# Two small changes in a fused attention and feed-forward kernel: eight early matmuls grouped by weight matrix, and the last half group of outputs cut into quarters

## The chip, the cores and the metric

One core of a Trainium2 chip; times are compared within one call, on one chip, unless it is said otherwise. The metric is device time in microseconds (us) of one execution. All executions compared here are fast, with a granted tensor-engine clock of 0.998 to 1.0. "Span" is the part of an execution that the profile covers; it is about 1.8 us shorter than the time.

## The reference

```python
def _attn_ref(q, k, v, g_norm):              # 8 batches, 8 heads, 576 tokens, head size 64
    kv = np.einsum('bhsd,bhse->bhde', k, v)
    out = np.einsum('bhsd,bhde->bhse', q, kv)
    rms = np.sqrt(np.mean(out * out, axis=-1, keepdims=True) + 1e-06)
    return (out / rms * g_norm).astype(np.float32)

def _moe_ref(x, w_a, w_b, w_out):            # 4608 tokens, width 512, inner width 1536
    a = x @ w_a
    b = x @ w_b
    return (a * b @ w_out).astype(np.float32)
# reference: x = attention output, heads side by side; result = _moe_ref(x, ...)
```

## The kernel before

Tokens go in 9 strips of 512. For each strip, 12 *units* (one per 128 columns of the inner width) each make four matmuls with w_a and four with w_b, one per K chunk of 128; ACT copies the a half to SBUF and DVE multiplies it with the b half. Then four groups of 12 matmuls with w_out make the outputs of 128 tokens each. The attention of later batches is spread between these matmuls. The contents of K chunk n of x are the heads 2n and 2n+1 ("pair n") of the attention.

POOL issues all loads of weights and of q, k and v, in the order of need. Everything up to batch 1 goes into buffers of its own:

```python
    for p in range(2, NP):
        load_pair(0, p)                       # q, k, v of a pair of heads of batch 0
    WC = 256
    for c in range(0, KC, 2):                 # first 256 columns of w_a, w_b: chunks 0-1, then 2-3
        for w, src in ((wa_t, wa_v), (wb_t, wb_v)):
            nc.gpsimd.dma_start(out=w[:, c : c + 2, 0:WC], in_=src[:, c : c + 2, 0:WC])
    for i in range(1, d_ff // WC):
        load_ab(i * WC, (i + 1) * WC)         # next 256 columns of both
    for i in range(FC):
        load_o(i)                             # w_out, 12 pieces
    for p in range(NP):
        load_pair(1, p)                       # batch 1
    load_late(2)
```

The start of the units, where the first part of the change lies (`first` is `mm(wa_t)` then `mm(wb_t)`; `rest` is `part_a` then `part_b`; `part_a` ends with the copy by ACT, `part_b` with the product by DVE):

```python
    u0 = Unit(0, 0, 2, 3)
    u1 = Unit(0, 1, 4, 5)
    u0.first((0, 1))
    A.pss(3, SS, (0,))
    A.pst(3, X[1], (0,))                      # x of pair 3, first half of the tokens, by DVE
    u1.mm(wa_t, (0,))
    A.pss(3, SS, (1,))
    A.pst(3, X[1], (1,))                      # second half
    u1.mm(wa_t, (1,))
    u1.mm(wb_t, (0, 1))
    u0.first((2,))
    u1.first((2,))
    u0.rest((3,))
    u1.rest((3,))
    u2 = Unit(0, 2, 0, 1)                     # "the next unit" below; takes columns 256 on
    ...
    ffn_o(0, 0, X[0])                         # first output group of strip 0
    pieces = [(1, h1), (1, h2), (2, h1), (2, h2), (3, h1), (3, h2)]
    for n, (g, fcs) in enumerate(pieces):     # half groups of output between the pairs of batch 1
        o_mm(0, g, O, fcs, halves=halves)
        ...
        if n < NP:
            A.qtr(n, 2)                       # transposes of q (line 200)
            A.kv(n) ...                       # K-times-V products of pair n (line 176)
```

And the end, the second part:

```python
    o_mm(last, 3, 5, range(FC), 0, hw)        # first half (256 columns) of the last group
    nc.vector.tensor_copy(o_sb[3][:, 0:hw], P[:, 5, 0:hw])
    store(r0, o_sb[3], 0, hw)                 # SP queue
    o_mm(last, 3, 6, range(FC), hw, d_model)  # second half
    nc.scalar.copy(o_end, P[:, 6, hw:])
    nc.scalar.dma_start(out=out[r0 : r0 + 128, hw:], in_=o_end)
```

Of the kernel before, what the change touches and what calls it, by code (L numbers as in the profile page):

```python
# [8 lines left out]
FP32 = mybir.dt.float32  # L9
# [6 lines left out]
def kernel(  # L16
# [11 lines left out]
    nc = tc.nc  # L28

    B, H, S, D = q.shape  # L30
    d_model = H * D
# [3 lines left out]
    FC = d_ff // 128  # L35
# [13 lines left out]
    def sb(shape, dt, name):  # L49
        return pool.tile(shape, dt, name=name, tag=name)  # L50

    wa_t = sb([128, KC, d_ff], BF16, "wa_t")
# [33 lines left out]
    x_last = x_last.rearrange("t (j p d) -> t j p d", j=2, p=NP)  # L86
    g_all = sb([128, D], FP32, "g_all")
    o_sb = [sb([128, d_model], FP32, f"osb{i}") for i in range(4)]
    o_end = sb([128, d_model // 2], FP32, "o_end")
    ident = sb([128, 128], BF16, "ident")  # L90
    ones = sb([128, 128], BF16, "ones")
    zeros = sb([128, STRIP], BF16, "zeros")
# [15 lines left out]
    P = psum.tile([128, 8, STRIP], FP32, name="P", tag="P")  # L108
# [48 lines left out]
    def product(o, lhsT, rhs, halves=False, **kw):  # L157
        for r in (slice(0, D), slice(D, 2 * D)) if halves else (slice(0, 2 * D),):
            nc.tensor.matmul(o[r], lhsT=lhsT[:, r], rhs=rhs, **kw)  # L159
# [236 lines left out]
    def store(t0, t, e0, e1, eng=nc.sync):  # L396
        i = 0
        while i < 128:
            b, j = divmod(t0 + i, S)
            if b < EARLY:  # L400
                c, p = divmod(j, EP)
                n = min(128 - i, EP - p)
                r0 = b * S + EC * p + c
                o = out[r0 : r0 + EC * (n - 1) + 1 : EC, e0:e1]
            else:
                n = min(128 - i, S - j)
                o = out[t0 + i : t0 + i + n, e0:e1]
            eng.dma_start(out=o, in_=t[i : i + n, e0:e1])
            i += n
# [3 lines left out]
    def o_mm(s, g, i, fcs, e0=0, e1=d_model, halves=False):  # L413
        for fc in fcs:
            product(
                P[:, i, e0:e1],
                abt[s % 2][fc][:, g * 128 : (g + 1) * 128],
                wo_t[:, fc, e0:e1],
                halves,
                start=(fc == 0),  # L420
                stop=(fc == FC - 1),
            )
# [98 lines left out]
    for p in range(1, NP):  # L521
        i = X[p % 2]
# [16 lines left out]
    u0 = Unit(0, 0, 2, 3)  # L539
    u1 = Unit(0, 1, 4, 5)  # L540
# [5 lines left out]
    A.pst(3, X[1], (1,))  # L546
    u1.mm(wa_t, (1,))
    u1.mm(wb_t, (0, 1))
    u0.first((2,))
    u1.first((2,))  # L550
    u0.rest((3,))
    u1.rest((3,))

    u2 = Unit(0, 2, 0, 1)
    u3 = Unit(0, 3, 2, 0)
# [33 lines left out]
    u0 = Unit(1, 0, 2, 3)  # L589
    u1 = Unit(1, 1, 4, 5)  # L590
# [55 lines left out]
    last = N_STRIP - 1  # L646
# [4 lines left out]
    hw = d_model // 2  # L651
    r0 = last * STRIP + 3 * 128
    o_mm(last, 3, 5, range(FC), 0, hw)
    nc.vector.tensor_copy(o_sb[3][:, 0:hw], P[:, 5, 0:hw])
    store(r0, o_sb[3], 0, hw)
    o_mm(last, 3, 6, range(FC), hw, d_model)
    nc.scalar.copy(o_end, P[:, 6, hw:])  # L657
    nc.scalar.dma_start(out=out[r0 : r0 + 128, hw:], in_=o_end)


# [28 lines left out]
```

## Time and profile before

| | before |
|---|---|
| time, median of 3 (range) | 313.72 us (313.65 to 313.87) |
| span of the profiled execution | 311.8 us |
| PE busy | 305.7 us, 98% |
| chain that ended last | PE 85%, DMA 8%, POOL 5% |
| first w_b matmul of chunk 2 | waits, starts at 16.65 us |
| line 176 of pairs 1 and 3 of batch 1 | start at 41.98 and 46.57 us |
| last copy by ACT | starts at 308.57 us |

PE is TensorE, PEld its weight loads. The chain that ended last is followed back from the last instruction, each time to what released it. It is the view to look at first here: PE is nearly always busy, but the chain tells where its work decides the time and where it merely fills the wait for something else. The lines themselves stand in the prediction.

### The profile page before, as it was taken

The numbers are of one execution on the slowest core, as the hardware profiler recorded it, in microseconds if no ns is written. First come the engines' busy times: TensorE is split into PE (matmuls) and PEld (weight loads), VectorE is DVE, ScalarE is ACT, GpSimd is POOL, SyncE is SP. The second block draws the span as 40 slices with busy tenths as digits, with TensorE's granted clock in tenths as the row PEclk, the third lists the DMA queues.
The fourth block names the chain that finished last, engine by engine and source line by source line (L and its number), as shares of the span: only waits on it lengthen the run. The fifth ranks groups of instructions, "written<-read, shape, count | busy, mean of one in ns | idle before, by whom it ended". The sixth has DMA issues, their size and how long they took to land.

```text
span 311.8 us, 5260 instructions
## 1 busy us (share of the span) xinstructions
PE 305.7 (98%) x2055; PEld 145.0 (47%) x2055; DVE 140.5 (45%) x234; ACT 116.9 (38%) x231; POOL 101.2 (32%) x123
## 2 busy tenths in 40 slices
PE   7999999999999999999999999999999999999995
PEld 3444474444454444544444445444444444444443
DVE  5544335458248603484386123752782143214321
ACT  3743255354255313561564033632651233123310
POOL 8944991193364640043646300221240000000000
PEclk9999999999999999999999999999999999999999
DMA  8999999999899799045997980073021200030002
GB/s 180 197 196 199 199 190 158 227 140 162 173 175 167 105 196 165 2 97 119 174 184 113 183 164 2 19 160 109 20 50 42 103 1 0 36 101 0 0 36 101
DMA packets 94254, 36.21 MB, mean 116 GB/s; under 512 B 64918, under 2 KB 89750, under 8 KB 94230
## 3 DMA queue, kind: packets, MB, share of 16 engines
q0 software_dynamic: 59120, 18.44, 54.3%
q1 hardware_dynamic: 34642, 16.87, 23.5%
q10 hardware_dynamic: 468, 0.57, 0.7%
q8 instruction: 16, 0.26, 0.3%
q14 instruction: 8, 0.07, 0.1%
HBM read 37.78 MB, written 12.98 MB: 163 GB/s over the span
## 4 chain that ended last, share of the span: by engine, by line
PE 85%; DMA 8%; POOL 5%; issue 1%; ACT 0%; POOLq 0%
PE P L358 53%; PE P L159 29%; DMA wb_t<-in_moe_w_b_dram 6%; DMA vt<-in_v_dram 2%; PE P L176 2%; PE P L292 1%; POOL qt L119 1%; POOL wo_t L134 1%; POOL kt L119 1%; POOL vt L119 1%; POOL wa_t L477 0%; POOL wb_t L477 0%; POOL wa_t L130 0%; PE P L200 0%; ACT o_end L657 0%
## 5 line engine op out<-in xcount | busy, mean ns | idle before, releaser
L376 DVE TENSOR_TENSOR ab<-P,asb 128x512 bf16<-128x512 f32 x108 | 74.4, 691 | 103.8 <-PE P L358 100.4
L358 PE MATMUL P<-xt,wb_t 128*128 128x512 bf16 x432 | 111.8, 379 | 0.3 <-DMA wb_t<-in_moe_w_b_dram 0.3
L358 PE MATMUL P<-xt,wa_t 128*128 128x512 bf16 x432 | 111.9, 379 | 0.0
L372 ACT CAST asb<-P 128x512 bf16<-128x512 f32 x108 | 62.9, 585 | 90.4 <-PE P L358 90.4
L159 PE MATMUL P<-wo_t,ab 128*128 128x512 bf16 (+2 forms) x462 | 95.7, 374 | 0.0
L159 PEld LDWEIGHTS <-ab 128*128 128x128 bf16 (+1 forms) x462 | 43.7, 99 | 48.5
L358 PEld LDWEIGHTS <-wb_t 128*128 128x128 bf16 x432 | 41.7, 98 | 50.6 <-DMA wb_t<-in_moe_w_b_dram 0.8
L358 PEld LDWEIGHTS <-wa_t 128*128 128x128 bf16 x432 | 41.8, 98 | 49.9 <-issue 0.2
L329 POOL TENSOR_TENSOR sqt<-rst,g_all 128x512 f32<-128x512 f32 (+1 forms) x24 | 25.0, 1043 | 85.2 <-ACT rst L322 85.2
L429 ACT COPY osb<-P 128x512 f32<-128x512 f32 x17 | 9.9, 585 | 70.2 <-PE P L159 65.6
L431 DVE COPY osb<-P 128x512 f32<-128x512 f32 x18 | 12.4, 691 | 44.9 <-PE P L159 44.9
L142 POOL DMA_DIRECT2D qs<-in_q_dram x12 | 19.8, 1653 | 0.7 <-issue 0.3
L313 DVE TENSOR_REDUCE sst<-sqt 128x8 f32<-128x512 f32 (+1 forms) x24 | 16.3, 680 | 1.7 <-ACT sqt L309 1.5
L338 DVE TENSOR_TENSOR qv<-P,sqt 128x512 bf16<-128x512 f32 x18 | 12.2, 680 | 0.0
L329 POOL TENSOR_TENSOR k_x<-rst,g_all 128x512 f32<-128x512 f32 x6 | 6.3, 1043 | 18.0 <-ACT rst L322 18.0
L322 ACT ACTIVATE rst<-sst,eps_t 128x8 f32<-128x8 f32 (+1 forms) x30 | 9.0, 300 | 7.1 <-DVE sst L313 6.8
L309 ACT ACTIVATE sqt<-P 128x512 f32<-128x512 f32 x18 | 10.5, 584 | 0.1
L241 DVE SCALAR_TENSOR_TENSOR xt<-P,g_col,rs 128x288 bf16<-128x288 f32 x16 | 7.5, 511 | 5.2 <-ACT rs L231 5.2
L134 POOL DMA_DIRECT2D wo_t<-in_moe_w_out_dram x12 | 6.4, 530 | 6.7 <-DMA wb_t<-in_moe_w_b_dram 3.2
L231 ACT ACTIVATE rs<-P,eps_t 128x576 f32<-128x576 f32 (+1 forms) x9 | 6.1, 688 | 3.8 <-PE P L159 3.5
L444 PE MATMUL P<-zeros 128*128 128x512 bf16 x17 | 6.0, 482 | 1.2 <-DVE eps_t L461 1.2
L139 POOL COPY gate<-qT 1x1 bf16<-1x1 bf16 x5 | 0.9, 176 | 16.8 <-DMA qT<-qs 16.7
(71 smaller groups left out, 130.7 us busy)
## 6 DMA issues: line engine op xcount, KB each, us to landing
out_dram<-osb SPq DMA_DIRECT2D x23, 256.0 KB, 2.0
qs<-in_q_dram POOLq DMA_DIRECT2D x12, 288.0 KB, 6.7
ktl<-in_k_dram POOLq DMA_DIRECT2D x6, 512.0 KB, 9.1
vtl<-in_v_dram POOLq DMA_DIRECT2D x6, 512.0 KB, 11.2
out_dram<-osb SPq DMA_DIRECT2D x13, 128.0 KB, 2.4
wo_t<-in_moe_w_out_dram POOLq DMA_DIRECT2D x12, 128.0 KB, 5.9
wa_t<-in_moe_w_a_dram POOLq DMA_DIRECT2D x5, 256.0 KB, 9.4
wb_t<-in_moe_w_b_dram POOLq DMA_DIRECT2D x5, 256.0 KB, 10.0
```

The source lines that it names most:

```text
L134: nc.gpsimd.dma_start(out=wo_t[:, i, :], in_=wo_v[:, i, :])
L142: nc.gpsimd.dma_start(out=d[:, hs, :], in_=q[b, hs].rearrange("h t d -> t h d"))
L159: nc.tensor.matmul(o[r], lhsT=lhsT[:, r], rhs=rhs, **kw)
L309: nc.scalar.activation(sqt[c % 3][r], self.by_head(c)[r], AF.Square)
L313: nc.vector.reduce_sum(sst[c % 3][r], sqt[c % 3][r].rearrange("t j p d -> t (j p) d"), axis=mybir.AxisListType.X,)
L329: nc.gpsimd.tensor_mul(sqt[c % 3][r].rearrange("t j p d -> t (j p) d"), rst[c % 3][r].unsqueeze(2).to_broadcast([n, H, D]), g_all[r].unsqu ...
L338: nc.vector.tensor_mul(t[r].rearrange("t (p j) d -> t j p d", j=2), self.by_head(c)[r], sqt[c % 3][r])
L358: nc.tensor.matmul(self.a if w is wa_t else self.b, lhsT=w[:, kc, self.fc * 128 : (self.fc + 1) * 128], rhs=xt[:, kc, t0 : t0 + STRIP], st ...
L372: nc.scalar.copy(self.t, self.a)
L376: nc.vector.tensor_mul(abt[self.s % 2][self.fc], self.b, self.t)
L429: nc.scalar.copy(t, P[:, i, :])
L431: nc.vector.tensor_copy(t, P[:, i, :])
```

## The change

The intent of part 1: at 16 us PE stood waiting for chunks 2 and 3 of w_b although w_a's were there, so do w_a's matmuls of both units first. The intent of part 2: at the end only the last copy and the last store are exposed, so make both smaller.

```diff
-    o_end = sb([128, d_model // 2], FP32, "o_end")
+    o_end = [sb([128, d_model // 4], FP32, f"o_end{i}") for i in range(2)]
...
-    u0.first((2,))
-    u1.first((2,))
-    u0.rest((3,))
-    u1.rest((3,))
+    u0.mm(wa_t, (2,))
+    u1.mm(wa_t, (2,))
+    u0.part_a((3,))
+    u1.part_a((3,))
+    u0.part_b((2, 3))
+    u1.part_b((2, 3))
...
-    o_mm(last, 3, 6, range(FC), hw, d_model)
-    nc.scalar.copy(o_end, P[:, 6, hw:])
-    nc.scalar.dma_start(out=out[r0 : r0 + 128, hw:], in_=o_end)
+    qw = hw // 2
+    for i, copy, eng in ((6, nc.vector.tensor_copy, nc.sync), (7, nc.scalar.copy, nc.scalar)):
+        e0 = hw + (i - 6) * qw
+        o_mm(last, 3, i, range(FC), e0, e0 + qw)
+        copy(o_end[i - 6], P[:, i, e0 : e0 + qw])
+        eng.dma_start(out=out[r0 : r0 + 128, e0 : e0 + qw], in_=o_end[i - 6])
```

## The prediction

> **What bounds the kernel now.** I read the page's busy shares first, then the chain that ended last, then the order of instructions on the tensor engine (PE) in the two places that the diff touches, then the landings of the loads behind them.
>
> From the page of the kernel before, busy times and the shares of the chain by engine:
>
> ```profile
> PE 305.7 (98%) x2055; PEld 145.0 (47%) x2055; DVE 140.5 (45%) x234; ACT 116.9 (38%) x231; POOL 101.2 (32%) x123
> ...
> PE 85%; DMA 8%; POOL 5%; issue 1%; ACT 0%; POOLq 0%
> ```
>
> PE is busy 98% of the span, yet only 85% of the chain is PE. The reader should ask where the other 15% lie, because there a faster PE gains nothing. The chain of waits in order of time answers (start us, length us, what):
>
> ```profile
> 11.34 7.67 DMA wb_t<-in_moe_w_b_dram
> 19.00 0.28 issue
> 19.29 10.40 DMA wb_t<-in_moe_w_b_dram
> ...
> 36.48 5.46 DMA vt<-in_v_dram
> 41.94 0.04 issue
> 41.98 0.38 PE P L176 x12
> ...
> 298.14 10.40 PE P L159 x60
> 308.55 0.02 issue
> 308.57 0.37 ACT o_end L657
> ```
>
> Up to 41.98 us the chain is loads and their issue by POOL, none of it PE. At 41.98 the K-times-V products of pair 1 of batch 1 (line 176) start right after their v data land at 41.94. From there to 308.55 it is PE without a break worth naming, then one copy and one store.
>
> The weight loads of PE around that point (timeline, weight loads only) show that the wait is real:
>
> ```profile
> 41.35 0.43 PEld L200 LDWEIGHTS <-qt 96*64 96x64 bf16 x12
> 41.69 0.11 PEld L176 LDWEIGHTS <-kt 96*64 96x64 bf16 x1
> 41.98 0.27 PEld L176 LDWEIGHTS <-kt 96*64 96x64 bf16 x11 [0.18 <-issue]
> ```
>
> The first k weights are in at 41.69, then PE stands. In pairs 2 and 3 line 176 starts 0.27 and 0.25 us after the transposes of line 200 (43.95 to 44.22, 46.32 to 46.57); here it is 0.51 (41.47 to 41.98). So PE already loses about 0.24 us to that load.
>
> The first place of the change, in the timeline of PE:
>
> ```profile
> 15.94 0.38 PE L358 MATMUL P<-xt,wa_t 128*128 128x512 bf16 x1
> 16.65 0.39 PE L358 MATMUL P<-xt,wb_t 128*128 128x512 bf16 x1 [0.33 <-DMA wb_t<-in_moe_w_b_dram]
> 16.88 0.38 PE L358 MATMUL P<-xt,wa_t 128*128 128x512 bf16 x1
> ```
>
> Matmuls of 512 columns start every 0.216 us here, so 16.65 should have been 16.16: the wait for chunks 2 and 3 of w_b costs 0.49 us of PE time (0.33 is only the part in which the pipeline was empty).
>
> The second place, the end of the timeline:
>
> ```profile
> 308.26 0.27 PE L159 MATMUL P<-wo_t,ab 128*128 128x256 bf16 x1
> 308.57 0.37 ACT L657 COPY o_end<-P 128x256 f32<-128x256 f32 x1 [4.62 <-PE P L159]
> 308.97 0.38 ACTq L658 DMA_DIRECT2D out_dram<-o_end  x1
> ```
>
> In windows of 0.1 us the bytes of that last store run from about 309.83 to 310.30; the span ends at 311.8.
>
> **What the Trainium skill says.** "TensorE: Matmul & The Clock Gate", section "Back-to-back issue gap", gives two answers for 128 columns: N/2.4 + 2.5 ns, thus 56 ns, for a lone stream, and about 81 ns where each matmul has its own weight load. This decides whether the quarters cost PE time. The trace has six such pairs (line 505, 96x128 weights, 128 columns): their weight loads start at 6.76, 6.81, 6.87, 6.92 and 6.98, so every 55 ns. It supports the lower figure, with a short sample. The page's 131 ns for 512 columns isn't what this trace has (216 ns).
> "DMA: Bandwidth & Descriptors", section "Anatomy of one DMA — SWDGE (gpsimd) path", says that most of a transfer's fixed cost is the confirmation of the last byte, whatever its size. The trace agrees in kind for the last store: 1.5 us pass from the last byte (310.3) to the end (311.8), and halving the store won't touch them. The same page, section "Specifications", puts the least row for full rate at 512 bytes; a quarter row is exactly 128 x 4 = 512 bytes. No store of the kernel before has such rows.
>
> **Part 1, the order of chunks 2 and 3.** No instruction is added or removed on any engine: eight matmuls go from a2 b2 a2 b2 a3 b3 a3 b3 (units 0, 0, 1, 1, 0, 0, 1, 1) to a2 a2 a3 a3 b2 b3 b2 b3. In the new order four w_a matmuls start at 15.94, 16.16, 16.37 and 16.59; the first w_b one at 16.80. The w_b load was issued at 9.87 and took 6.7 us, so it lands at about 16.57 and was usable at 16.65: no wait any more. The eighth starts at 17.45 and the next unit could start at 15.94 + 8 x 0.216 = 17.67 instead of 18.18, 0.51 earlier.
> That unit takes columns 256 to 512 of w_a. They were issued at 10.58 and took 7.1, so land at about 17.68, and its weight load would stand ready at 17.45. I put its start at 17.75: the local gain is 0.43 us. The next ones are in time: the same columns of w_b land at 19.00 for 19.47.
> Then 0.43 us travels with PE through the units of strip 0, and is lost in steps. The last piece of w_out is issued at 32.57 and takes about 4.9, lands near 37.5; PE wants it at 37.81 before (35.44 + 11 x 0.216) and at 37.38 after. So about 0.3 is left. v of pair 0 of batch 1 is issued at 34.53, takes 5.2, lands at 39.73; line 176 used it at 39.74. So at most 0.05 is left. And v of pair 1 lands at 41.94 whatever PE does: POOL waits only for earlier transfers in those 42 us, never for a compute engine, and each load has a buffer of its own. PE arrives earlier and waits longer. Worth on the path: 0.00.
>
> **Part 2, the quarters.** Removed: 12 matmuls of 256 columns, one copy of 256 columns on ACT, one store of 128 KB. Added: 24 matmuls of 128 columns, two copies of 128 columns (DVE, ACT), two stores of 64 KB (SP, ACT).
> PE: the 24 matmuls of 256 columns before start from about 305.75 to 308.26, 109 ns apart, so the half to be split starts at 307.06. With 24 x 55.8 ns the last one starts at 307.06 + 23 x 0.0558 = 308.34 and, with the 218 ns of line 505's form, ends at 308.56 against 308.53: +0.03.
> First quarter: ends at 307.06 + 11 x 0.0558 + 0.22 = 307.89; DVE is free since 307.68 and needs about 0.29 (0.425 for 256 columns, 0.691 for 512); SP, free since 308.04, issues at about 308.25, bytes are through by 309.4. It is beside the second quarter and off the path.
> Second quarter, on the path: the ACT copy takes 0.372 for 256 columns and 0.212 for 64, so about 0.265 for 128: -0.11. The issue and the 0.86 us from issue to first byte stay. The bytes took about 0.47 us at about 345 GB/s between ramps; half of them 0.19 plus ramps, say 0.27: -0.20. The last 1.5 us stay.
> Sum of part 2: +0.03 - 0.11 - 0.20 = -0.28 us. Sum of both: -0.28 us, 0.1% of the time. 313.72 - 0.28 = 313.44.
>
> **Rivals.**
> First: the front gain survives, since the landings at 39.73 and 41.94 move too. For it: the chain takes its releases from semaphore events and "issue" is named for the 0.18 us at 41.98, so the release by v is inferred. Against it: landing and start agree to 0.04 us, and the DMA engines moved 190 to 200 GB/s in nearly every us from 6 to 40, so the loads have no slack to give. It would make 313.72 - 0.43 - 0.28 = 313.0.
> Second: weight loads bound the quarters at 81 ns a matmul. Then they take 24 x 0.081 = 1.94 us instead of 1.31, +0.63, and the time is about 314.05. Against it stand line 505's 55 ns and its overlapping loads (98 ns each at 55 ns spacing); for it, that only six of them were seen.
> Third: rows of 512 bytes are slower per byte, or two stores in flight delay each other, so the transfer saves nothing: 313.6. The first quarter's bytes should be gone about 0.3 us before the second's begin, which speaks against the latter.
>
> **Range and chances.** The centre is 313.4. Half of the first rival and repeats a little lower give 312.95; the third with ordinary scatter (the three runs before span 0.22 us), or a part of the second, gives 313.8. A change of 2% would be 6.3 us; all that is touched, 0.5 us at the front and the last 1.3 us of PE time with its tail, comes nowhere near it.
>
> **What would show it.** Right: the wait at 16.65 gone, the next unit at about 17.7 to 17.75 with a short wait for w_a; line 176 of pair 1 of batch 1 again at 41.9 to 42.0, with about 0.3 to 0.6 us of idle PE before it and at pair 0; the matmuls from there to the end of the same length; last quarters 55 ns apart; the ACT copy at 0.26 to 0.28 us. Wrong: line 176 of pair 1 starting near 41.5, quarters 80 ns or more apart, or a last store whose bytes take 0.4 us or more.

## The result, and the profile after

| | before | after |
|---|---|---|
| time, median of 6 (range) | 313.63 us (313.48 to 313.87) | 313.25 us (313.10 to 313.62) |
| ratio of the fast runs | | 0.9989, 95% interval 0.9976 to 1.0002 |
| span of the profiled execution | 311.8 us | 311.5 us |

A ratio here is the mean time of one kernel's fast runs over the mean of the other's from the same rounds, so it is not quite the ratio of the medians. 0.38 us by the medians is near the 0.28 us forecast, but the interval just includes 1: these repeats can't say much about a quarter of a microsecond. The traces can, because they resolve 0.01 us and because the long middle of the program takes the same time in each of them.

The chain that ended last, of the changed kernel (start us, length us, what):

```profile
11.39 7.43 DMA wb_t<-in_moe_w_b_dram
...
36.58 5.26 DMA vt<-in_v_dram
41.84 0.04 issue
41.89 0.38 PE P L176 x12
...
308.51 0.27 ACT o_end L664
```

It has the same shape. Until 41.89 us it is loads and their issue; v of pair 1 lands at 41.84 (before: 41.94) and line 176 starts 0.05 us later. So the start of the PE part moved by 0.09 us because the load landed earlier in this execution, not because PE had arrived earlier.

The reordered eight, in the timeline of PE of the changed kernel:

```profile
16.06 1.27 PE L358 MATMUL P<-xt,wa_t 128*128 128x512 bf16 x4
17.17 1.02 PE L358 MATMUL P<-xt,wb_t 128*128 128x512 bf16 x4
18.04 1.03 PE L358 MATMUL P<-xt,wa_t 128*128 128x512 bf16 x4
```

The wait for w_b is gone, and the next unit starts 1.98 us after the first of the eight (16.06 to 18.04) against 2.24 before (15.94 to 18.18). But eight matmuls at 0.216 us are 1.73 us: there is a new gap of 0.25 us among the first four, which last 1.27 us instead of 3 x 0.216 + 0.38 = 1.03. The experiments below say what it is.

The wall at 42 us shows in the weight loads of the changed kernel:

```profile
41.27 0.43 PEld L200 LDWEIGHTS <-qt 96*64 96x64 bf16 x12
41.61 0.11 PEld L176 LDWEIGHTS <-kt 96*64 96x64 bf16 x1
41.89 0.26 PEld L176 LDWEIGHTS <-kt 96*64 96x64 bf16 x11 [0.17 <-issue]
```

The first k weights are in, and PE stands until v lands, as before. The end of the timeline of the changed kernel:

```profile
307.84 0.29 DVE L664 COPY o_end<-P 128x128 f32<-128x128 f32 x1 [0.24 <-PE P L159]
...
308.51 0.27 ACT L664 COPY o_end<-P 128x128 f32<-128x128 f32 x1 [4.65 <-PE P L159]
308.81 0.38 ACTq L665 DMA_DIRECT2D out_dram<-o_end  x1
```

And the bytes of the last store in windows of 0.2 us (the columns after the window are busy time of PE, PEld, DVE, ACT and POOL, the clock, the DMA share and GB/s), first of before, then of after:

```profile
309.80:310.00 0.20, 0.00 (x0) 0.00 (x0) 0.00 (x0) 0.00 (x0) 0.00 (x0) 1.00 0.60 205
310.00:310.20 0.20, 0.00 (x0) 0.00 (x0) 0.00 (x0) 0.00 (x0) 0.00 (x0) 1.00 1.04 353
310.20:310.40 0.20, 0.00 (x0) 0.00 (x0) 0.00 (x0) 0.00 (x0) 0.00 (x0) 1.00 0.31 98
```

```profile
309.60:309.80 0.20, 0.00 (x0) 0.00 (x0) 0.00 (x0) 0.00 (x0) 0.00 (x0) 1.00 0.42 125
309.80:310.00 0.20, 0.00 (x0) 0.00 (x0) 0.00 (x0) 0.00 (x0) 0.00 (x0) 1.00 0.70 200
310.00:310.20 0.20, 0.00 (x0) 0.00 (x0) 0.00 (x0) 0.00 (x0) 0.00 (x0) 1.00 0.01 3
```

The last byte leaves about 0.3 us earlier on the clock of the execution, of which 0.09 is the earlier start at 42 us.

### The profile page after: what moved, and what is told of

The parts are those of the page before. It is cut to its first block, busy times and chain, and to the rows that moved or that the text cites. A ratio compares the mean times of both kernels' runs of the same rounds, so it can differ in the third digit from the quotient of the medians.

```text
span 311.5 us, 5288 instructions
## 1 busy us (share of the span) xinstructions
PE 306.4 (98%) x2067; PEld 145.7 (47%) x2067; DVE 140.7 (45%) x235; ACT 117.0 (38%) x231; POOL 101.2 (32%) x123
## 4 chain that ended last, share of the span: by engine, by line
PE 86%; DMA 7%; POOL 5%; issue 1%; ACT 0%; POOLq 0%
PE P L358 54%; PE P L159 29%; DMA wb_t<-in_moe_w_b_dram 6%; DMA vt<-in_v_dram 2%; PE P L176 2%; PE P L292 1%; POOL qt L119 1%; POOL wo_t L134 1%; POOL kt L119 1%; POOL vt L119 1%; POOL wb_t L477 0%; POOL wa_t L477 0%; POOL wa_t L130 0%; PE P L200 0%; POOL ident masks.py:199 0%
## 5 line engine op out<-in xcount | busy, mean ns | idle before, releaser
L159 PE MATMUL P<-wo_t,ab 128*128 128x512 bf16 (+3 forms) x474 | 95.7, 368 | 0.0
```

Of the source, the lines that this page charges most:

```text
L159: nc.tensor.matmul(o[r], lhsT=lhsT[:, r], rhs=rhs, **kw)
```

## The experiments

Theory 1: up to about 46 us the time is set by the landing of loads, which doesn't depend on PE (a *wall* below is such a load: PE waits for it, however early it comes); what part 1 wins is waited away there, and all that the change wins is the shorter tail. Rivals: the front gain survives; the walls are not loads; the tail wins nothing.

Twelve kernels were run. Executions of one kernel scatter by 0.2 to 1 us, as much as the effects, so each verdict rests on the times *and* on four starts in the trace of the profiled execution:

| kernel | first of the eight | next unit | difference | line 176, pair 1 | line 176, pair 3 | time of this execution | time less pair 3 |
|---|---|---|---|---|---|---|---|
| before | 15.94 | 18.18 | 2.24 | 41.98 | 46.57 | 313.64 | 267.07 |
| after | 16.06 | 18.04 | 1.98 | 41.89 | 46.49 | 313.26 | 266.77 |
| front_only | 16.34 | 18.08 | 1.74 | 42.00 | 46.59 | 313.64 | 267.05 |
| tail_only | 16.38 | 18.10 | 1.72 | 41.87 | 46.47 | 313.24 | 266.77 |
| noload_before | 15.93 | 17.87 | 1.94 | 41.76 | 46.51 | 313.55 | 267.04 |
| noload_front | 16.06 | 18.04 | 1.98 | 41.94 | 46.69 | 313.74 | 267.05 |
| noload2_before | 16.07 | 18.02 | 1.95 | 41.53 | 46.28 | 313.31 | 267.03 |
| noload2_front | 16.39 | 18.37 | 1.98 | 41.88 | 46.63 | 313.66 | 267.03 |
| noload2_both | 16.07 | 18.05 | 1.98 | 41.56 | 46.31 | 313.06 | 266.75 |
| noload2_chunk2 | 16.40 | 18.13 | 1.73 | 41.64 | 46.39 | 313.18 | 266.79 |
| early2 | 16.46 | 18.86 | 1.97 + 0.43 | 42.38 | 47.13 | 313.92 | 266.79 |
| late2 | 16.19 | 18.05 | 1.86 | 41.94 | 46.54 | 313.80 | 267.26 |
| tail_one_mm | 15.96 | 17.93 | 1.97 | 41.84 | 46.44 | 313.55 | 267.11 |
| o_ahead | 16.07 | 17.80 | 1.73 | 42.49 | 46.66 | 313.49 | 266.83 |

The last column is the tool: by pair 3 the loads are behind, and what follows is PE alone up to the tail. The six kernels with the old tail read 267.03 to 267.07, the six with the new one 266.75 to 266.83 (late2, with work added behind pair 3, and tail_one_mm, with a tail of its own, apart). Two things vary from one execution to the next for reasons outside the change: the start of the eight (15.93 to 16.46), and the landing of v. In the traced executions, one per kernel, they account for nearly all of the scatter of the times; the other executions have no trace, and the cause of the two was not followed further.

### front_only and tail_only: each part alone

`front_only` is before with only the reordering of the diff, `tail_only` before with only the quarters.

> Part 1 alone. Theory 1 (the loads of batch 1 set the time at 42 us, so what PE wins before is waited away): time within 0.1 us of before, line 176 of pair 1 of batch 1 starting at 41.8 to 42.0 in the trace, the unit after the reordered eight about 0.25 us earlier relative to the first w_a matmul of chunk 2 than in before. Rival (the front gain survives to the end): 0.25 us faster than before.

Measured: 313.47 us median (313.39 to 313.64, 5 runs) against 313.46 of before (313.21 to 313.62, 9 runs), ratio 1.0000 (0.9986 to 1.0014). Line 176 of pair 1 starts at 42.00, as theory 1 has it. The next unit started 0.50 us earlier relative to the first of the eight than in before, 1.74 instead of 2.24, but in this trace the first of them had itself waited for w_a (it started at 16.34 where 15.98 was due), so that everything later was ready when asked for. On the clock the next unit started 0.10 us earlier than in before (18.08 against 18.18) and line 176 of pair 1 0.02 us later.

The chain of waits names v in before and after, but not here, nor in tail_only, late2 and tail_one_mm below: there it gives the last 0.03 or 0.04 us before line 176 as "issue" and goes back along PE's own work. That v is the wall in these too is read from two other things. Line 176 of pair 1 starts 0.47 to 0.49 us after the transposes of line 200, against 0.25 or 0.26 in the kernels without batch 1's loads. And v was issued at 36.50 here and took 5.5 us, so it landed at about 42.0, where line 176 started.

> Part 2 alone. Theory 1: all of the gain, 0.25 to 0.35 us faster than before. Rival (the front carries the gain): 0.1 us or less.

Measured: 313.41 us median (313.24 to 313.51, 5 runs), ratio 0.9997 (0.9985 to 1.0010): 0.05 us by the medians, 0.09 by the means, which is a miss against the 0.25 to 0.35 expected. In the trace, however, time less pair 3 is 266.77, exactly that of the changed kernel, 0.28 to 0.30 below front_only and before. So the tail's gain is in the trace, and medians of five executions with ranges of 0.27 and 0.41 us don't resolve it. It also shows that the old order doesn't always wait at 16 us: here the eight began at 16.38, w_b was there, and the next unit started 1.72 us later with no gap.

### noload_before and noload_front: batch 1's loads taken away

Both read batch 0's q, k and v tiles in place of batch 1's, which are not loaded; batch 1's rows are wrong. Old tail in both.

```diff
-    for p in range(NP):
-        load_pair(1, p)
...
-                kk, vv, rows = kt[self.b], vt[self.b], [EP] * EC
+                kk, vv, rows = kt[0], vt[0], [EP] * EC
...
-                        qt[self.b][:, 2 * p + j, c, :],
+                        qt[0][:, 2 * max(p, 1) + j, c, :],
```

(and the same `max(p, 1)` for k and v, as pair 0 of batch 0 lies elsewhere)

> Before without the q, k and v loads of batch 1; batch 1 takes the q, k, v tiles of batch 0 that are long there, so batch 1's rows are wrong on purpose. Theory 1: the wait at line 176 goes (0.24 us at pair 1, up to 0.1 at pair 0), time 0.2 to 0.4 us below before. Rival (the release by the v load was only inferred and isn't the cause): same time as before.

Measured: 313.85 us median (313.20 to 314.20, 5 runs), ratio 1.0008 (0.9996 to 1.0021): no gain, so as a prediction of the time it failed. The wait at pair 1 did go (41.50 to 41.76 is 0.26 us from the transposes, against 0.51 in before). The chain of waits of noload_before shows what took its place:

```profile
32.39 5.46 DMA wo_t<-in_moe_w_out_dram
37.85 0.04 issue
37.89 0.38 PE P L159
```

The last piece of w_out lands at 37.85, and PE waits for it there. In before that piece was issued at 32.57 and took about 4.9 us, so it landed at about 37.5, in time for the 37.8 at which PE wanted it. Here PE wanted it earlier, at 37.5 (35.14 + 11 x 0.216), and it took 5.5 us. So this is not a wall that had stood hidden in before: PE came earlier and the piece came later. The edit itself may have had a part in the latter, because it also moved later loads forward: the first q of batch 2 was issued at 41.50 in before, and at 33.08 here, right behind the last piece of w_out. Whether that slowed the piece isn't shown.

> The same with part 1 alone added. Theory 1: with those loads gone the front gain reaches the end, 0.25 us below noload_before. Rival (the gain is lost at some other wait, for example the K and V loads of batch 2 near 60 us): the same as noload_before.

Measured: 313.71 us median (313.20 to 313.86, 5 runs), ratio 1.0005 (0.9993 to 1.0018). Within the scatter equal to noload_before, which looks like the rival, but the rival named K and V of batch 2 near 60 us, and the trace has the wait at w_out again (the piece was issued only at 32.94, took 5.1 us and landed at 38.03; the matmul starts at 38.08).

### noload2_before, noload2_front, noload2_both, noload2_chunk2: both walls taken away

As above, and strip 0 takes w_out chunks 0 to 3 in place of 8 to 11, so that it needs no late piece (strip 0 is wrong as well; all of w_out is still loaded, and batch 2's loads come as early as in noload_before):

```diff
-                wo_t[:, fc, e0:e1],
+                wo_t[:, fc if s else fc % 8, e0:e1],
```

> As noload_before, and strip 0 takes w_out chunks 0 to 3 in place of 8 to 11, so that it doesn't need the last pieces of w_out either (strip 0 and batch 1 wrong on purpose; all of w_out is still loaded). In the two runs without batch 1's loads PE waited for the last piece of w_out at 37.9 to 38.1 instead. Theory 1, widened (any load that ends near 38 to 42 us is a wall for PE): the waits from 37 to 47 us go and the time falls by 0.25 to 0.4 us below before. Rival (the walls aren't loads): same as before.

Measured: 313.20 us median (312.99 to 313.31, 5 runs) against 313.53 of before (313.17 to 313.96, 9 runs), ratio 0.9988 (0.9976 to 1.0001). 0.33 us less by the medians, within the 0.25 to 0.4 expected, though the interval just includes 1. In the profiled execution the part between the next unit and pair 3 took 28.26 us against 28.39 in before, and the next unit itself came 0.16 us earlier, as w_b landed sooner. So the walls are these loads, but only 0.13 us of the 0.33 are theirs in the trace; that the total fell into the range is partly luck. Their net cost is smaller than I had thought: a PE held at pair 1 makes up 0.16 us by pair 3 (4.59 us from pair 1 to pair 3 in before, 4.75 here). The timeline of noload2_before shows why:

```profile
41.24 0.58 ACT L429 COPY osb<-P 128x512 f32<-128x512 f32 x1 [0.86 <-PE P L159]
41.87 1.49 PE L159 MATMUL P<-wo_t,ab 128*64 128x512 bf16 x12
```

The matmuls after the products of pair 1 write the place that ACT is copying the previous output group from, and start 0.05 us after that copy ends (41.82), 0.34 us after line 176; in all six kernels without batch 1's loads they start 0.04 to 0.06 us after it. In before the copy ended at 42.03, and the matmuls started at 42.16, 0.18 us after line 176. So behind the wall of v stands a wait for ACT of 0.16 us that the wall covers.

> The same with part 1. Theory 1: what part 1 gains at 18 us now reaches the end, whatever it is in the trace: 0.25 us if w_b lands as late as in before (16.6), nothing if it lands at 16.35 as it did in noload_before, as the third matmul of the new order then waits for x of pair 3 (ready at about 16.7). Time against noload2_before: 0 to 0.25 us less, and equal to the difference of the starts of the next unit in the two traces within 0.1 us. Rival: no connection between the two.

Measured: 313.52 us median (313.32 to 313.66, 5 runs), 0.32 us *more* than noload2_before, outside the range of 0 to 0.25 us less. The second half of the expectation held: the next unit started at 18.37 against 18.02, 0.35 us later, and pair 1 (41.88 against 41.53), pair 3 (46.63 against 46.28) and the time of that execution (313.66 against 313.31) are all 0.35 later. Over the four kernels without walls, pair 1 starts 23.51 us and pair 3 28.26 us after the next unit, each time. With walls the first of these was 23.77 to 23.92. So without walls the front does pass to the end one to one, and with them it doesn't. (What passed here is a late start, not a gain of part 1.)

What made the front late is an early start that came 0.32 us later in this execution (16.39 against 16.07), and that part 1's order did not use the time: the difference stays 1.98, where the old order in the same situation (tail_only, 16.38) needed only 1.72.

> The same with both parts. Theory 1: 0.28 us below noload2_front, the tail alone, with less scatter than in the kernels whose loads set the start. Rival (the tail saves nothing end to end, as tail_only's medians suggest): the same as noload2_front.

Measured: 313.12 us median (313.06 to 313.33, 5 runs), 0.40 us below noload2_front by the medians. Between the two profiled executions the difference is 0.60 us (313.66 and 313.06): 0.32 of it stands at the next unit already (18.37 and 18.05) and at pair 3 (46.63 and 46.31), and the remaining 0.28 comes after pair 3, which is the tail's gain. How much of the 0.40 is the start can't be said, as the other runs have no trace. Less scatter, which was expected too, was not seen: the five runs span 0.27 us, those of front_only 0.25. The chain of waits of this kernel also names what the reordered eight wait for:

```profile
15.23 0.51 ACT rs L231
...
15.76 0.95 DVE xt L241 x2
16.71 0.04 issue
16.76 3.40 PE P L358 x15
```

Line 241 is the DVE instruction that writes x of pair 3, which is K chunk 3. It ends at 16.71, and 0.05 us later the matmul goes on. In the new order the third matmul already needs chunk 3; in the old one the fifth does.

> As noload2_both, but the eight matmuls in the order a2 a2 b2 b2 a3 a3 b3 b3 (units 0 and 1 each), which asks for w_b and for x of pair 3 about when each is ready. Theory: the third and fifth matmuls wait 0.1 us or less each, the next unit starts 1.75 to 1.85 us after the first of the eight instead of 1.98, 0.1 to 0.2 us below noload2_both. Rival (x of pair 3 isn't what the third matmul waits for): same as noload2_both.

```diff
     u0.mm(wa_t, (2,))
     u1.mm(wa_t, (2,))
+    u0.mm(wb_t, (2,))
+    u1.mm(wb_t, (2,))
     u0.part_a((3,))
     u1.part_a((3,))
-    u0.part_b((2, 3))
-    u1.part_b((2, 3))
+    u0.part_b((3,))
+    u1.part_b((3,))
```

Measured: 313.00 us median (312.84 to 313.18, 5 runs), ratio 0.9982 (0.9968 to 0.9996), 0.12 us below noload2_both by the medians and 0.14 by the means, as expected, but the runs of the two overlap. Its timeline of PE:

```profile
16.40 0.60 PE L358 MATMUL P<-xt,wa_t 128*128 128x512 bf16 x2
16.84 0.59 PE L358 MATMUL P<-xt,wb_t 128*128 128x512 bf16 x2
17.27 0.59 PE L358 MATMUL P<-xt,wa_t 128*128 128x512 bf16 x2
17.70 0.59 PE L358 MATMUL P<-xt,wb_t 128*128 128x512 bf16 x2
```

No gap, and the next unit follows at 18.13, 1.73 us after the first, a little less than the 1.75 to 1.85 expected. This execution began late, so that it doesn't test the wait for w_b (the wait for x it does test: noload2_front began as late and had it); but o_ahead below has the same order with an early start (16.07), and its difference is 1.73 too, where the old order there needed 1.95 and part 1's 1.98. So chunk 2 first is the order that waits for neither.

### early2 and late2: two extra matmuls ahead of the walls, and behind them

The changed kernel with `dummy(2, 7)`, two matmuls on zeros of 0.216 us each, either right before `u2 = Unit(0, 2, 0, 1)` or after the attention of batch 1. Both give correct results.

> The changed kernel with two extra 512-column matmuls on zeros (0.43 us of PE) right after the eight reordered ones, before the third unit. Correct result. Theory 1 (walls of loads near 38 to 42 us): PE waits 0.35 us less there, so 0.0 to 0.15 us above the changed kernel. Rival (PE sets the time from 18 us on): 0.43 us above it.

> The changed kernel with the same two matmuls after the attention of batch 1, behind the last wall (near 53 us). Correct result. Both theories: the full 0.43 us above the changed kernel; theory 1: 0.3 to 0.43 us above early2, rival: the same as early2. By the time less the start of line 176 of pair 1: 271.8 here, against 271.37 in early2.

Measured, against 313.53 of before (313.16 to 313.90, 9 runs): early2 313.64 us median (313.42 to 313.92, 5 runs), late2 313.80 (313.58 to 313.99, 5 runs). The order is that of theory 1, but the two are only 0.16 us apart by the medians and 0.12 by the means, not 0.3 to 0.43, and early2 lies about 0.4 above the changed kernel's 313.25 of another call (0.5 by the ratios to before, 1.0004 and 0.9989). Theory 1 expected 0.0 to 0.15, the rival 0.43: by its time, early2 is a miss for theory 1. Only the trace, of the slowest of its five runs, says why. In the timeline of PE of early2:

```profile
18.43 0.59 PE L444 MATMUL P<-zeros 128*128 128x512 bf16 x2
...
42.38 0.35 PE L176 MATMUL P<-vt,kt 96*64 96x64 bf16 x12
```

The eight began at 16.46 here, 0.40 later than in after, so the next unit came at 18.86; 23.52 us later stands line 176 of pair 1, the interval of the kernels without walls. PE reached pair 1 when v was there. In after the next unit came at 18.04, so without a wait PE would have reached line 176 of pair 1 at 41.55 (23.51 us later), and it started at 41.89: 0.34 us of slack; the late start of 0.40 had used that up, and this execution had nothing left for the dummies. So the slack ahead of the wall is not a fixed 0.35 us. Whether the four other runs of early2 began late as well isn't known. In late2 it was there: the wall held pair 1 at 41.94, and time less pair 3 is 267.26, the 0.43 us above the others within 0.06. The traces of the pair are consistent with theory 1; its times don't decide, and early2's lean to the rival.

### tail_one_mm: which term of the tail

```diff
-        o_mm(last, 3, i, range(FC), e0, e0 + qw)
-        copy(o_end[i - 6], P[:, i, e0 : e0 + qw])
+        if i == 6:
+            o_mm(last, 3, 6, range(FC), hw, d_model)
+        copy(o_end[i - 6], P[:, 6, e0 : e0 + qw])
```

> The changed kernel, but the last half group is one set of 256-column matmuls again; its copy and its store stay cut in two, by DVE with SP and by ACT with ACT, both at once. Theory (the tail's gain is the shorter copy plus fewer bytes behind the last matmul): the copy's 0.11 us stay, the bytes' 0.2 us are lost as both stores run together; time less the start of line 176 of pair 1 is 271.5 to 271.6 against 271.37 of the changed kernel and 271.65 of before. Rival (halving each store is what counts, together or not): 271.35.

Measured: 313.55, 313.68 and 313.48 us, and one execution of 317.68 at the full clock that no other shows and that is left out here; it is why the computed ratio, 1.0034 (0.9985 to 1.0084), says nothing. By the trace, time less pair 1 is 313.55 - 41.84 = 271.71, above the 271.5 to 271.6 expected and above before's 271.66: no gain at all. From its timeline:

```profile
308.43 0.29 DVE L665 COPY o_end<-P 128x128 f32<-128x128 f32 x1 [0.89 <-PE P L159]
308.76 0.27 ACT L665 COPY o_end<-P 128x128 f32<-128x128 f32 x1 [4.95 <-DVE o_end L665]
```

The two copies did not run at once: the trace names DVE's copy as what ACT's waited for, and bank 6 of PSUM (the memory that the matmuls write, in banks) is all that the two share. The Trainium skill, "PSUM — Partial Sum Buffer", section "PSUM bank collisions raise a hardware error", says that two engines must not access one bank in the same partitions at a time, reads included, and that software has to order them; the 0.33 us from 308.43 to 308.76 fit that order. In the changed kernel the quarters lie in two banks, and the first one's copy (307.84) runs beside the second one's matmuls; that one bank would forbid this follows from the page and was not tried.

The run was meant to tell the shorter copy from the fewer bytes. It can't, but it does show that both are kept with the matmuls whole: relative to pair 3 (46.44) ACT's copy starts at 262.32, 0.32 us later than in before, and yet the execution ends only 0.04 us later (267.11 against 267.07). The copy took 0.27 us, and in windows of 0.05 us the bytes of the two stores ran one after the other, the last in 7 or 8 windows. So about 0.28 us were saved behind the last copy's start here too, as the rival had it; the missing gain is the wait of one copy for the other. The two terms are read from the traces of before and after instead.

### o_ahead: a version meant to be faster

```diff
-    ffn_o(0, 0, X[0])
-    pieces = [(1, h1), (1, h2), (2, h1), (2, h2), (3, h1), (3, h2)]
+    for g in range(2):
+        o_mm(0, g, X[g], h1)
+    for g in range(2):
+        o_mm(0, g, X[g], h2)
+        o_out(0, g, X[g])
+    pieces = [(2, ()), (2, range(4)), (2, range(4, 8)), (2, range(8, FC)), (3, h1), (3, h2)]
```

together with the order of noload2_chunk2 and the new tail.

> A version meant to beat both, correct: the changed kernel with the eight matmuls as a2 a2 b2 b2 a3 a3 b3 b3, and with the second output group of strip 0 wholly before batch 1's attention (its first half before the first group's second half), the third group in three pieces of four. PE then asks for the last piece of w_out 1.3 us later and for batch 1's v of pairs 0 to 2 1.3, 0.9 and 0.4 us later. Theory 1: the waits from 37 to 45 us go, 0.2 to 0.4 us below the changed kernel, line 176 of pair 3 near 46.4. Rival (the walls were not the limit, or the new order makes waits of its own): the same as the changed kernel or slower.

Measured: 313.49 us median (313.33 to 314.17, 5 runs) against 313.53 of before, ratio 1.0002 (0.9990 to 1.0015). The waits for loads at pairs 0 and 1 did go (line 176 of pair 1 comes at 42.49, 0.25 us after its transposes), but two waits of its own came instead:

```profile
42.00 0.44 PE L159 MATMUL P<-qT,kvb 128*64 128x288 bf16 x4 [0.16 <-DVE qT L207]
...
46.17 0.44 PE L159 MATMUL P<-qT,kvb 128*64 128x288 bf16 x4 [0.19 <-DVE qT L207]
```

With pieces of four matmuls in place of six, PE comes to the product with q before DVE has copied it out; the chain of waits has ACT's output copy and its two copies of K-times-V ahead of DVE's copy at the first of them. Pair 3 starts at 46.66, later than in after (46.49). A piece of PE work moved ahead of a load is missing later as cover for the engines' copies. It beats neither kernel.

## Why the prediction was right

The forecast was 313.4 us with 312.95 to 313.8; 313.25 was measured. Of the 0.38 us between the two traced executions (313.64 and 313.26) 0.30 lie behind pair 3, in the tail; the other 0.08 are there because v landed earlier in that execution, which is luck. Point by point:

- **Part 1 is worth 0.00 on the path: right.** With part 1 (after, front_only) pair 3 starts at 46.49 and 46.59, without it (before, tail_only) at 46.57 and 46.47. Without the loads in the way, the start of the next unit passes to the end one to one (28.26 us to pair 3 in all four noload2 kernels). The first rival, 313.0, needed a gain that passes, and none is seen. The gain that these traces had to pass on was small (the next unit 0.14 us earlier on the clock in after than in before, 0.02 in front_only than in tail_only); what carries the point is that PE stood at pair 1 already in before, 0.51 us from the transposes to line 176 where 0.26 do without the load, so that coming earlier only lengthens the wait.
- **The local gain of 0.43 us: wrong in size, and so is the step that made it.** I had the eight matmuls run without a gap from 15.94 on, then a short wait for w_a of the next unit. There is no such wait, but the third matmul waits about 0.25 us for x of pair 3 from DVE, which I had not checked. The gain at the next unit relative to the first of the eight is 2.24 - 1.98 = 0.26 us, and only where w_b is late: the old order needed 1.95 and 1.94 where w_b landed a little sooner, and 1.72 where the whole start was late (tail_only), against 1.98 of part 1 in a start as late (noload2_front). So there part 1 gains nothing or loses up to 0.26. The walls hid this error, as they would have hidden the gain.
- **The steps of the loss:** that the last piece of w_out would already take part of it didn't happen in the changed kernel (21.24 us from the next unit to line 200 of pair 0 in before and in after), as PE came only 0.14 us earlier. A wait at that piece was seen only without batch 1's loads, where the piece landed later (37.85 and 38.03 against about 37.5). Pairs 0 and 1 were the walls, as said: line 176 of pair 0 came 0.39 us after its transposes in after, 0.32 in before.
- **Part 2, 0.28 us: right.** By time less pair 3 it is 0.30 between before and after, 0.28 between front_only and tail_only and between noload2_front and noload2_both. The terms, relative to pair 3: the ACT copy starts at 262.02 instead of 262.00 (+0.02, forecast +0.03); it takes 0.266 us instead of 0.372 (-0.11, as forecast); the bytes are seen in 8 windows of 0.05 us instead of 11, about -0.15 against -0.20 forecast. The 1.5 us from the last byte to the end did stay: 310.3 to 311.8 before, 310.0 to 311.5 after. (The page that the prediction names for this describes transfers issued by POOL; the last store is ACT's, so it is the trace that carries the point.) The few hundredths that are left lie after the last byte, at the limit of what the span (given to 0.1 us) resolves.
- **The second rival, 81 ns a matmul, is out:** five starts of the last quarter lie within 0.22 us, so 55 ns each. **The third** is partly there: the last store peaked at 307 GB/s in windows of 0.05 us against 389 before, which took about 0.05 us of the forecast 0.20. The prediction named bytes that take 0.4 us or more as a sign of being wrong, and 8 windows of 0.05 us are just 0.4. But the same windows give 0.55 for the store before, which the prediction had at 0.47 by coarser ones; so the transfer did get shorter.
- **Other signs:** the next unit at 17.7 to 17.75 with a short wait for w_a did not come (18.04, no wait); line 176 of pair 1 at 41.89, the quarters at 55 ns and the copy at 0.266 us did.

## What to carry to other kernels

Before valuing a gain inside the kernel, follow the chain of waits to the next point where the engine waits for a load: ahead of such a wall a faster compute engine only waits longer, and behind it another wait may stand that it covers, so that taking it away wins less than the wait was long. Taking a load away also moves the loads behind it: look at their landings too. When an instruction is moved forward, check every input that it reads, not only the one whose wait is to go. And where repeats scatter as much as the effect, subtract a late common milestone in the trace: here that turned a scatter of 0.86 us (313.06 to 313.92) into groups that agree within 0.1 us.

## What the Trainium skill lacked or had wrong

- "TensorE: Matmul & The Clock Gate", section "Back-to-back issue gap": about 81 ns (128 columns) and 131 ns (512 columns) a matmul for a stream with one weight load each. These runs show 55 ns and 216 ns, which is the page's formula for an isolated matmul (N/2.4 + 2.5 ns), though these matmuls stand in streams with a weight load each.
- "DMA: Bandwidth & Descriptors", section "Specifications", puts full rate from 512 bytes on. The last store with rows of 512 bytes peaked at 307 GB/s (64 KB in about 0.40 us), with rows of 1,024 bytes at 389 GB/s (128 KB in about 0.55 us). It isn't only that a short store is mostly ramps: divided by the busy share of the DMA engines, the windows give about 286 GB/s after and 337 before (an estimate from their sums), 15% less. Row length and size of the store changed together, so which of them it is isn't shown. Half the bytes saved 0.15 us and not half of the time; the lower rate is about 0.035 us of that (64 KB at 286 and at 337 GB/s), the rest lies in the ramps.
- No page that I read has a way to see a quarter of a microsecond behind run-to-run scatter; time less the start of line 176 of pair 3 gave 267.03 to 267.07 for the six kernels with the old tail and 266.75 to 266.83 for the six with the new one, where their medians overlap.
